# A fixed list of TensorE's products replaced by a choice made step by step, in a fused attention and two-layer kernel

## The chip, the cores and the metric

The kernel runs on one core of a Trainium2 chip. The metric is device microseconds of one execution, the median of several. Matrix products run on TensorE (PE), elementwise work on VectorE (DVE), ScalarE (ACT) and GpSimd (POOL), and transfers are issued by SyncE (SP).

## What is computed

Three stages stand behind one another, with 2304 tokens (4 batches of 576), 8 heads of 64 and a model width of 512:

```python
kv  = einsum('bhsd,bhse->bhde', k, v)          # linear attention
out = einsum('bhsd,bhde->bhse', q, kv)
x   = out / sqrt(mean(out**2) + 1e-6) * g_norm
x   = ((x @ w_a) * (x @ w_b)) @ w_out          # 512 -> 1536 -> 512
h   = x @ w_in                                 # 512 -> 1024
solu = h * softmax(h)
y   = layernorm(solu) * g_ln @ w_out2          # 1024 -> 512
```

The weights arrive as float64 and are turned into pairs of float32r numbers, high and low, on the chip.

## The kernel before: how the work is ordered

The kernel is written in Python that emits instructions engine by engine. Each engine runs its own queue in the order of emission, so the order in which the Python code calls the helpers is the order on the chip. To choose that order the code keeps a small model of time (`Order`, L45 to L92): every operation is given an assumed duration, every engine a time at which it is free, and chains of operations (`od.chain`) are emitted when the model's clock reaches them. The model sets the order alone. On the chip each instruction waits for its real inputs.

**Attention.** For a batch there are four key-value products (`att_kv`, tiles `pkv`, L468) and five token tiles. A token tile is a product with q (`att_1`, tile `o`, L491), a square on ScalarE (`sq`, L516), a copy (`x`, L508), a sum on VectorE (`r`, L518), a power on GpSimd (`r`, L521), a multiplication on VectorE (`x`, L522), and then a transposition on TensorE (`att_2`, tile `t`, L533) that ScalarE and VectorE copy out as `xh` (L546) and `xl` (L547). The tiles `pkv`, `o` and `t` share two PSUM buffers.

**Weights.** A chunk of w_a, w_b or w_out (512 columns; the three of one `f` are `w f,0`, `w f,1`, `w f,2`) is loaded as int64 into one of three buffers, decoded by one step on ScalarE (L286) and five on VectorE (L289, L292, L298, L303, L307), and split by ScalarE (`wh`, L365) and GpSimd (L366, `wl` L367). There are places for six split chunks, so for two values of `f`.

**First layer.** The width of 1536 is cut into 12 parts `f`, the tokens into six blocks `j` of 384. A block of `f` is eight groups of three products for w_a and w_b (`ab_items`, L563 to L565), an elementwise product `a` on ScalarE and VectorE (L612, L613), a split into `gh` (ScalarE, L615) and `gl` (GpSimd, L616), and four groups of three products with w_out (`y_items`, L643), whose sum goes to `ya`: a copy on ScalarE (L654) or an addition on VectorE (L656).

**Order of the first layer.** Before the change it is a list, `main` (L830 to L841): for each block the products of f=0 and f=1 and then the products with w_out of both, summed in one PSUM tile; from f=2 on one f after the other, the products with w_out of a block behind the next block's first products. The loop (L858 to L906) takes the list's next item when the model says that it is ready, and mixes attention in by a credit that `att_cost` (L847) works out from the attention due for the next block. Loads of weights stand between loads of attention by the table `FIRST` (L197): how many weight chunks may be asked for after how many attention loads.

**Second layer.** It runs behind that as a pipeline over 18 token tiles (`run_h`, `run_t`, `run_o`, L726 to L827), which the change leaves as it is.

Of the kernel before, what the change touches and what calls it, by code (L numbers as in the profile page):

```python
# [9 lines left out]
F32 = mybir.dt.float32  # L10
# [7 lines left out]
P = 128  # L18
# [95 lines left out]
def attention_moe_moe_kernel(ctx: ExitStack, tc, kv_in, kv_tail, q_in, g_norm, w1, w_in, w_out2, g_ln, out):  # L114
# [155 lines left out]

    def rank_of(k):

        return {("w", 0, 0): 1.5, ("w", 0, 1): 1.5, ("w", 0, 2): 2.5, ("w", 1, 0): 2.5}.get(k, 5)

    def decode(k):
        nm = f"{k[0]}{k[1]}_{k[2]}"
        slot, raw, when = arrived.pop(k)
        su, sf = R_U.take(), R_F.take()
        w = raw.bitcast(U32).rearrange("p (n two) -> p n two", two=2)
        u = ph1.tile([P, CH], F32, tag="u", name="u_" + nm)  # L280
        f = ph1.tile([P, CH], F32, tag="f", name="f_" + nm)
# [13 lines left out]

        def b3():

            nc.vector.scalar_tensor_tensor(  # L298
                out=fb, in0=w[:, :, 1], scalar=0xC0000000, in1=ub, op0=ALU.bitwise_and, op1=ALU.bitwise_or
            )  # L300

        def b4():
            nc.vector.tensor_scalar(out=ub, in0=fb, scalar1=0xFF800000, scalar2=None, op0=ALU.bitwise_and)  # L303

        def b5():

# [12 lines left out]
        od.chain(  # L319
            [("A", 0.52, a), ("V", 0.34, b1), ("V", 0.34, b2), ("V", 0.6, b3), ("V", 0.34, b4), ("V", 0.6, b5),  # L320
             (None, 0, freed), (None, 0, last)],
            rank=rank_of(k), t=max(od.now, when),
        )

    def store(k, f, u, su, sf, t):

        what, x, y = k
        if what == "o" and x >= 3:
            wf[x] = w2.tile([P, CH], F32, tag=f"wf{x}", name=f"wf{x}", bufs=1)

# [23 lines left out]
        if what == "o":  # L354
            g = gl_sb[:, x:x + 1]
            gwh[x], gwl[x] = hi, lo
            ops = [
                ("G", 1.23, lambda: nc.gpsimd.tensor_tensor(out=f, in0=f, in1=u, op=ALU.add)),
                ("A", 0.6, lambda: nc.scalar.activation(out=hi, in_=f, func=AF.Copy, scale=g)),
                ("V", 0.66, lambda: nc.vector.scalar_tensor_tensor(  # L360
                    out=lo, in0=f, scalar=g, in1=hi.bitcast(F32), op0=ALU.mult, op1=ALU.subtract)),
            ]
        else:
            ops = [
                ("A", 0.52, lambda: nc.scalar.copy(out=hi, in_=f)),  # L365
                ("G", 1.23, lambda: nc.gpsimd.tensor_tensor(out=f, in0=f, in1=hi.bitcast(F32), op=ALU.subtract)),  # L366
                ("G", 1.23, lambda: nc.gpsimd.tensor_tensor(out=lo, in0=f, in1=u, op=ALU.add)),  # L367
            ]

        def done(t):  # L370
# [79 lines left out]

    def run_back():
        _, b, t, x, sx = back.pop(0)
        od.pe(0.44, lambda: att_2(b, t, x, sx))

    def att_kv(b, p):
        (slot, t, _), tl = arrived.pop(("kv", b, p)), arrived["tail", b, 0][1]
# [28 lines left out]
    def att_1(b, t):  # L485
# [25 lines left out]
        def done(when):  # L511
# [9 lines left out]
            ("G", 1.65, lambda: nc.gpsimd.tensor_tensor(out=r[0:n], in0=r[0:n], in1=mhalf[0:n], op=ALU.pow)),  # L521
            ("V", 0.6, lambda: nc.vector.tensor_tensor(  # L522
                out=x[0:n], in0=x[0:n], in1=r[0:n].unsqueeze(2).to_broadcast([n, H, D]), op=ALU.mult)),
            (None, 0, done),
        ], rank=rank, t=od.now + 0.88 + 0.2)
# [46 lines left out]
    def ab_items(f, j):  # L572
# [3 lines left out]
        def ready(m, kt):  # L576
            t = w_ready.get(("w", f, m), INF)
            if m == kt == 0:
                t = max(t, tokens_ready((j + 1) * NB), ps_ready())
                if not (R_A.ok() and R_G.ok()):  # L580
                    return INF
            return t

        def run(m, kt):
            started.add(f)
            if m == kt == 0:
                st["slot"], st["ps"] = ps_tile(f"ab{f}_{j}")
# [12 lines left out]
        def post():  # L600
# [5 lines left out]
            def done(t):  # L606
# [2 lines left out]
                g_ready[f, j] = t  # L609

            od.chain([
                ("A", 0.41, lambda: nc.scalar.copy(out=a, in_=ps[:, 0, 0:NB])),  # L612
                ("V", 0.5, lambda: nc.vector.tensor_tensor(out=a, in0=ps[:, 1, 0:NB], in1=a, op=ALU.mult)),  # L613
                ps_done(st["slot"]),
                ("A", 0.41, lambda: nc.scalar.copy(out=gh, in_=a)),  # L615
                ("G", 0.96, lambda: nc.gpsimd.tensor_tensor(out=gl, in0=a, in1=gh.bitcast(F32), op=ALU.subtract)),  # L616
                (None, 0, done),
            ], t=od.now + G3 + 0.1)
# [4 lines left out]
    def y_items(fs, j):  # L623
# [10 lines left out]
        def run(f, m2, i):  # L634
# [198 lines left out]
    n_two = len(main)  # L833
    prev = None
    for f in range(2, NF1):
        for j in range(NBLK):
            main += ab_items(f, j)
            if prev:
                main += y_items(*prev)
            prev = [f], j  # L840
    main += y_items(*prev)  # L841

    n_block = n_two // NBLK
    AHEAD = 4
    SLACK = 3.0

    def att_cost(n):  # L847

        t = 0.44 * sum(b * S + i * P < n for _, b, i, *_ in back)
        for w, b, i in front:  # L850
            if b * S + (i * P if w == "t" else 0) < n:
                t += 1.32 if w == "t" else 0.75
        return t

    loads()
    decode_more()
    credit, n_main = 0.0, 0
    while main:  # L858
        od.until(od.now)
        loads()  # L860
        decode_more()
        if w2 is None and not att_left[0]:
# [6 lines left out]
        cost, ready, run = main[0]  # L869
        can = ready() <= od.now  # L870
        b_can = back and back[0][0] <= od.now and R_PA.ok()
        f_can = front_ready() <= od.now
        if (b_can or f_can) and (credit > 0 or not can):
            t0 = od.now
            after_back[0] = b_can
            if b_can:
                run_back()
            else:
                run_front()
            if can:  # L880
                credit -= od.now - t0
            continue
        if can:
# [7 lines left out]
            main.pop(0)  # L891
            n_main += 1
            od.pe(cost, run)
            split_more()
            continue
        if f_can or b_can:
            continue

        if todo_h and len(main) <= 8 and h_ready(todo_h[0]) <= od.now and len(held) < 2:
            run_h(todo_h.pop(0))  # L900
            continue
        nxt = [t for t in (ready(), front_ready(), back[0][0] if back and R_PA.ok() else INF) if t < INF]
        if od.events:
            nxt.append(od.events[0][0])
        assert nxt, "stuck"
        od.now = max(od.now, min(nxt))  # L906
    while todo_o:
        od.until(od.now)
        ahead = len(todo_o) - len(todo_h)
# [83 lines left out]
```

## Time and profile before

| what | value |
|---|---|
| median of three executions | 742.25 us (742.07 to 742.89) |
| the profiled execution | 742.4 us |
| its span in the profile | 740.5 us |
| TensorE busy | 719.1 us, 97% of the span |
| VectorE, GpSimd, ScalarE busy | 477.2, 283.1, 247.2 us |
| TensorE's granted clock, mean | 0.993 of full speed |

The span is the time from the first to the last instruction on the core. The profiled execution's own time is 1.9 us longer than its span, and that part lies outside what the trace shows. A matmul's busy time covers its whole pass through the array, and passes overlap, so that TensorE can be counted busy while its rate is below the best. The granted clock is given as a share of 2.4 GHz, where 0.50 is 1.2 GHz.

### The profile page before, as it was taken

What the parts mean: (1) busy time and instruction counts of PE and PEld (TensorE: products, weight loads), DVE (VectorE), ACT (ScalarE), POOL (GpSimd) and SP (SyncE); (2) the same over time, 40 slices, a digit from 0 to 9 for tenths busy, and PEclk for the clock granted to TensorE, in tenths of its full rate; (3) what the DMA queues carried; (4) which work ended last, traced back from release to release, by engine and by line L of the source; (5) the groups of instructions that cost most, each with busy time, mean ns of one, the idle gap of its engine ahead of it and who ended that gap; (6) DMA issues with size and microseconds to landing.
All of it is one profiled execution on the core that took longest, in us unless ns stands there. A gap on an engine that the chain in (4) does not pass through costs nothing.

```text
span 740.5 us, 10433 instructions
## 1 busy us (share of the span) xinstructions
PE 719.1 (97%) x4184; PEld 670.9 (91%) x4184; DVE 477.2 (64%) x662; ACT 247.2 (33%) x458; POOL 283.1 (38%) x271
## 2 busy tenths in 40 slices
PE   5799999899999999999999999999999999999998
PEld 5679999889999999999999999999878888888887
DVE  3992554699959595959594939466695544536350
ACT  4574555433333232323231313224532221212221
POOL 2792424575656464535352525221420111111110
PEclk9799999999999999999999999999999999999999
DMA  8715050023121212121211100000000000000001
GB/s 305 284 66 192 23 212 2 29 89 110 58 86 58 86 58 85 58 86 58 86 58 57 58 29 29 1 1 0 1 1 29 26 19 29 14 30 15 28 26 46
DMA packets 16336, 46.81 MB, mean 63 GB/s; under 512 B 2080, under 2 KB 3360, under 8 KB 16288
## 3 DMA queue, kind: packets, MB, share of 16 engines
q1 hardware_dynamic: 16288, 46.15, 17.2%
q8 instruction: 33, 0.54, 0.3%
q14 instruction: 15, 0.12, 0.0%
HBM read 41.42 MB, written 4.72 MB: 62 GB/s over the span
## 4 chain that ended last, share of the span: by engine, by line
PE 87%; DVE 7%; ACT 2%; POOL 2%; issue 2%; DMA 1%; SPq 0%; ACTq 0%; POOLq 0%
PE y L643 18%; PE ab L563 12%; PE ab L564 12%; PE ab L565 12%; PE h L565 4%; PE out L565 4%; PE h L563 4%; PE out L564 4%; PE out L563 4%; PE h L564 4%; PE t L792 2%; PE o L491 2%; PE pkv L468 2%; DMA kv<-in_kv 1%; DVE f_w L298 1%
## 5 line engine op out<-in xcount | busy, mean ns | idle before, releaser
L563 PE MATMUL ab<-xh,wh_w 128*128 128x384 f32 x576 | 195.3, 339 | 0.0
L564 PE MATMUL ab<-xl,wh_w 128*128 128x384 f32 x576 | 193.0, 335 | 0.4 <-DVE xl L547 0.4
L565 PE MATMUL ab<-xh,wl_w 128*128 128x384 f32 x576 | 193.0, 335 | 0.1
L616 POOL TENSOR_TENSOR gl<-a,gh 128x384 fp32r<-128x384 f32 x72 | 75.6, 1050 | 150.9 <-ACT gh L615 150.9
L656 DVE TENSOR_TENSOR ya<-y,ya 128x768 f32<-128x768 f32 x120 | 111.3, 949 | 6.6 <-PE y L643 5.1
L563 PEld LDWEIGHTS ab<-xh,wh_w 128*128 128x128 f32 x576 | 108.5, 188 | 1.0 <-issue 0.3
L564 PEld LDWEIGHTS ab<-xl,wh_w 128*128 128x128 f32 x576 | 108.5, 188 | 0.8 <-DVE xl L547 0.8
L565 PEld LDWEIGHTS ab<-xh,wl_w 128*128 128x128 f32 x576 | 108.4, 188 | 0.4 <-POOL wl_w L367 0.4
L643 PE MATMUL y<-gh,wh_w 128*128 128x384 f32 x288 | 97.7, 339 | 1.9 <-ACT gh L615 1.9
L643 PE MATMUL y<-gl,wh_w 128*128 128x384 f32 x288 | 96.8, 336 | 2.3 <-POOL gl L616 2.2
L613 DVE TENSOR_TENSOR a<-ab,a 128x384 f32<-128x384 f32 x72 | 39.8, 553 | 88.2 <-ACT a L612 88.2
L643 PE MATMUL y<-gh,wl_w 128*128 128x384 f32 x288 | 96.3, 334 | 0.0
L366 POOL TENSOR_TENSOR f_w<-f_w,wh_w 128x512 f32<-128x512 f32 x36 | 50.3, 1396 | 62.3 <-ACT wh_w L365 62.3
L612 ACT COPY a<-ab 128x384 f32<-128x384 f32 x72 | 34.4, 477 | 102.0 <-PE ab L565 101.9
L770 DVE TENSOR_REDUCE st<-h 128x1 f32<-128x1024 f32 x18 | 22.0, 1220 | 67.1 <-PE h L565 67.0
L643 PEld LDWEIGHTS y<-gl,wh_w 128*128 128x128 f32 x288 | 54.1, 188 | 3.6 <-POOL gl L616 3.6
L563 PE MATMUL h<-winh,yh 128*128 128x512 f32 x144 | 56.2, 390 | 0.8 <-DVE u L772 0.8
L643 PEld LDWEIGHTS y<-gh,wh_w 128*128 128x128 f32 x288 | 54.1, 188 | 2.9 <-ACT gh L615 2.6
L565 PE MATMUL h<-winh,yl 128*128 128x512 f32 x144 | 56.2, 391 | 0.0
L564 PE MATMUL h<-winl,yh 128*128 128x512 f32 x144 | 56.1, 389 | 0.0
L643 PEld LDWEIGHTS y<-gh,wl_w 128*128 128x128 f32 x288 | 54.1, 188 | 0.0
L615 ACT CAST gh<-a 128x384 fp32r<-128x384 f32 x72 | 37.0, 513 | 48.2 <-DVE a L613 47.9
(92 smaller groups left out, 1157.4 us busy)
## 6 DMA issues: line engine op xcount, KB each, us to landing
raw_w<-in_w SPq DMA_DIRECT2D x36, 512.0 KB, 3.2
kv<-in_kv SPq DMA_DIRECT2D x16, 512.0 KB, 4.5
out<-ot SPq DMA_DIRECT2D x17, 256.0 KB, 2.0
raw_i<-in_w_in SPq DMA_DIRECT2D x8, 512.0 KB, 3.2
raw_o<-in_w_out SPq DMA_DIRECT2D x8, 512.0 KB, 3.3
q<-in_q SPq DMA_DIRECT2D x12, 288.0 KB, 4.7
tail<-in_kv_tail SPq DMA_DIRECT2D x4, 256.0 KB, 5.4
q<-in_q SPq DMA_DIRECT2D x4, 192.0 KB, 5.0
```

The lines of the kernel that those rows point to most:

```text
L366: ("G", 1.23, lambda: nc.gpsimd.tensor_tensor(out=f, in0=f, in1=hi.bitcast(F32), op=ALU.subtract)),
L468: nc.tensor.matmul(o, lhsT=k, rhs=v, start=c == 0, stop=c == SC)
L563: nc.tensor.matmul(o, lhsT=ah, rhs=bh, start=first, stop=False)
L564: nc.tensor.matmul(o, lhsT=ah, rhs=bl, start=False, stop=False)
L565: nc.tensor.matmul(o, lhsT=al, rhs=bh, start=False, stop=last)
L612: ("A", 0.41, lambda: nc.scalar.copy(out=a, in_=ps[:, 0, 0:NB])),
L613: ("V", 0.5, lambda: nc.vector.tensor_tensor(out=a, in0=ps[:, 1, 0:NB], in1=a, op=ALU.mult)),
L615: ("A", 0.41, lambda: nc.scalar.copy(out=gh, in_=a)),
L616: ("G", 0.96, lambda: nc.gpsimd.tensor_tensor(out=gl, in0=a, in1=gh.bitcast(F32), op=ALU.subtract)),
L643: nc.tensor.matmul(o, lhsT=x[:, s], rhs=y, start=f == fs[0] and n == 0, stop=f == fs[-1] and n == 2)
L656: op = ("V", 0.87, lambda: nc.vector.tensor_tensor(out=dst, in0=src, in1=dst, op=ALU.add))
L770: ("V", 1.13, lambda: nc.vector.tensor_reduce(out=nmax, in_=ps, axis=AX.XY, op=ALU.max, negate=True)),
```

## The change

The list is gone. The loop now keeps, for each f, the blocks whose products with w_a and w_b are still to do (`ab`), the block begun (`busy`), and a queue `yq` of blocks whose products with w_out are still to do. At each step it takes the next block of the oldest unfinished f, or, where that block is not ready in the model, the next block of the f behind it. The products with w_out come when they are ready and two further blocks are behind them, or when nothing else is ready. Attention gets a credit of twice the time of each other item (`ATT`). The products with w_out of f=0 and f=1 are no longer summed in one PSUM tile: f=0 is copied, f=1 is added on VectorE. The buffers of `a` and `gh`/`gl` are claimed at a block's last group and not at its first. The model's durations are new, so are the ranks of the first chunks, and three entries are added to `FIRST` and two moved.

```diff
-    FIRST = {0: 1, 9: 3, 14: 4, 17: 5, 21: 6}
+    FIRST = {0: 1, 9: 3, 14: 4, 18: 5, 22: 6, 27: 7, 32: 8, 36: 9}
...
-        return {("w", 0, 0): 1.5, ("w", 0, 1): 1.5, ("w", 0, 2): 2.5, ("w", 1, 0): 2.5}.get(k, 5)
+        return {("w", 0, 0): 1.5, ("w", 0, 1): 1.5, ("w", 0, 2): 2.5, ("w", 1, 0): 3.5, ("w", 1, 1): 3.5}.get(k, 5)
...
-            [("A", 0.52, a), ("V", 0.34, b1), ("V", 0.34, b2), ("V", 0.6, b3), ("V", 0.34, b4), ("V", 0.6, b5),
+            [("A", 0.6, a), ("V", 0.5, b1), ("V", 0.5, b2), ("V", 0.95, b3), ("V", 0.5, b4), ("V", 0.85, b5),
...
-    G3 = 0.4885
+    G3 = 0.52
...
-                if not (R_A.ok() and R_G.ok()):
-                    return INF
+            if m == 1 and kt == NP - 1 and not (R_A.ok() and R_G.ok()):
+                return INF
...
-                if f < 2:
+                if f < 1:
...
-    G2 = 0.6515
+    G2 = 0.68
...
-    main = []
-    for j in range(NBLK):
-        main += ab_items(0, j) + ab_items(1, j) + y_items([0, 1], j)
...
+    ab = [[ab_items(f, j) for j in range(NBLK)] for f in range(NF1)]
+    yq, busy = [], []
+    ATT = 2.0
+
+    def next_ab():
+
+        if busy:
+            return busy[0]
+        two = [f for f in range(NF1) if ab[f]][0:2]
+        for n, f in enumerate(two):
+            if (n == 0 or len(ab[f]) > len(ab[two[0]])) and ab[f][0][0][1]() <= od.now:
+                busy.append(ab[f].pop(0))
+                yq.append([f, NBLK - 1 - len(ab[f]), None])
+                return busy[0]
+        return None
...
+        a, y = next_ab(), next_y()
+        if a and a[0][1]() > od.now:
+            a = None
+
+        it = y if y and (len(y) < 4 or not a or len(yq) > 2) else a
...
-        if (b_can or f_can) and (credit > 0 or not can):
+        if (b_can or f_can) and (credit > 0 or not it):
...
+            c, ready, run = it.pop(0)
             if att_left[0]:
-
-                j = n_main // n_block
-                credit += cost * max(
-                    att_cost((j + 2) * NB) / max(G3 * (n_block - n_main % n_block) - SLACK, G3),
-                    att_cost(NT) / max(G3 * (n_two - n_block - n_main), G3),
-                )
...
+                credit += ATT * c
```

What this moves is seen in the engines' queues. **ScalarE, third and fourth token tile of batch 0** (`sq_3`, `x_3`: the fourth tile's square and copy; `xh` out of `t_0`: the first tile's transposition). Before:

```order
L516 ACTIVATE sq_3_267<-o_3_261 128x512
L520 ACTIVATE r_2_251<-r_2_251 128x8
L546 ACTIVATE xh_106<-t_0_274,gn 128x4x128
L365 CAST wh_w_1_286<-f_w_1_163 128x512
L508 COPY x_3_266<-o_3_261 128x512
L520 ACTIVATE r_3_268<-r_3_268 128x8
L546 ACTIVATE xh_106<-t_1_294,gn 128x4x128
```

and now:

```order
L516 ACTIVATE sq_3_266<-o_3_260 128x512
L508 COPY x_3_265<-o_3_260 128x512
L520 ACTIVATE r_2_251<-r_2_251 128x8
L546 ACTIVATE xh_106<-t_0_274,gn 128x4x128
L516 ACTIVATE sq_4_288<-o_4_282 64x512
L508 COPY x_4_287<-o_4_282 64x512
L546 ACTIVATE xh_106<-t_1_297,gn 128x4x128
```

The copy `x_3`, which frees a PSUM buffer, stood behind `xh` and a weight split, and stands directly behind `sq_3` now; the split of chunk `w 0,1` goes behind the second tile's `xh`.

**VectorE, second and third token tile of batch 0** (`xl` out of `t_1` and of `t_2`, or `x_2`, `x_3`: the tiles' products with their factors; `u_w_2`, `f_w_2`: decoding of the chunk `w 0,2`). Before:

```order
L547 SCALAR_TENSOR_TENSOR xl_107<-t_1_294,gn,xh_106 128x4x128
L518 TENSOR_REDUCE r_4_308<-sq_4_307 64x8
L298 SCALAR_TENSOR_TENSOR f_w_2_219<-raw_w_2_151,u_w_2_218 128x512
L522 TENSOR_TENSOR x_3_266<-x_3_266,r_3_268 128x512
L547 SCALAR_TENSOR_TENSOR xl_107<-t_2_317,gn,xh_106 128x4x128
```

and now:

```order
L547 SCALAR_TENSOR_TENSOR xl_107<-t_1_297,gn,xh_106 128x4x128
L518 TENSOR_REDUCE r_3_267<-sq_3_266 128x8
L518 TENSOR_REDUCE r_4_289<-sq_4_288 64x8
L289 TENSOR_SCALAR u_w_2_220<-u_w_2_220 128x512
L547 SCALAR_TENSOR_TENSOR xl_107<-t_2_335,gn,xh_106 128x4x128
L292 TENSOR_SCALAR u_w_2_220<-u_w_2_220 128x512
L522 TENSOR_TENSOR x_3_265<-x_3_265,r_3_267 128x512
L298 SCALAR_TENSOR_TENSOR f_w_2_221<-raw_w_2_151,u_w_2_220 128x512
```

The decoding step at L298 and the product `x_3` stood ahead of the third tile's `xl` and stand behind it now.

**TensorE, the last blocks of f=0 and f=1** (`ab_5_1439` is block 5 of f=1 before; `ab_2_1321` and `ab_3_1386` are blocks 2 and 3 of f=1 in the change; `y_5` and `y_2` are products with w_out of those blocks, or of block 5 of f=0). Before:

```order
L565 MATMUL ab_5_1439<-xh_109,wl_w_1_487 128x384
L643 MATMUL y_5_0_1481<-gh_5_1433,wh_w_2_372 128x384
...
L643 MATMUL y_5_1_1495<-gh_5_1433,wl_w_2_373 128x384
L643 MATMUL y_5_0_1481<-gh_5_1478,wh_w_2_553 128x384
...
L563 MATMUL ab_0_1532<-xh_106,wh_w_0_1416 128x384
```

and now:

```order
L565 MATMUL ab_2_1321<-xh_106,wl_w_1_663 128x384
L644 MATMUL y_5_0_1364<-gh_5_1293,wh_w_2_432 128x384
...
L644 MATMUL y_5_1_1373<-gh_5_1293,wl_w_2_433 128x384
L563 MATMUL ab_3_1386<-xh_109,wh_w_0_521 128x384
...
L644 MATMUL y_2_0_1422<-gh_2_1361,wh_w_2_741 128x384
```

Before, 12 products lay between the end of f=1's last block and the first product that reads its `gh` (`gh_5_1478`). Now 12 products with w_out of another set and the 24 of a further block lie between a block and its own products with w_out.

Two counts hold for the whole queue of TensorE. Its first 588 instructions (as they are issued) are the same set before and after: all attention, f=0 and f=1 whole, and block 0 of f=2. From instruction 589 on, block 1 of f=2, the order is the same to the end.

## Rows read from the trace of the kernel before

**Rows 1.** The page's head and its part 1, TensorE's line.
```profile
span 740.5 us, 10433 instructions
...
PE 719.1 (97%) x4184; PEld 670.9 (91%) x4184; DVE 477.2 (64%) x662; ACT 247.2 (33%) x458; POOL 283.1 (38%) x271
```

**Rows 2.** The chain that ended last, blocks of y: start us, us, what.
```profile
182.65 2.08 PE y L643 x12
...
519.61 2.08 PE y L643 x12
```

**Rows 3.** Busy time by stretch: us, busy (instructions) of each engine, PEclk, DMA share, GB/s.
```profile
20.00:54.00 34.00, 28.88 (x220) 23.84 (x218) 33.18 (x46) 20.50 (x48) 28.59 (x19) 0.85 0.48 175
```

**Rows 4.** TensorE in order of time: start us, us, instruction, [idle before it].
```profile
22.23 0.66 PE L533 MATMUL t<-ident,x 128*128 128x128 f32 x4 [1.77 <-ACT x L508]
...
25.79 1.11 PE L533 MATMUL t<-ident,x 128*128 128x128 f32 x4 [1.75 <-DVE xl L547]
...
29.34 0.69 PE L564 MATMUL ab<-xl,wh_w 128*128 128x384 f32 x1 [0.35 <-DVE xl L547]
...
143.61 0.45 PE L643 MATMUL y<-gh,wh_w 128*128 128x384 f32 x1 [1.54 <-ACT gh L615]
...
150.91 0.33 PE L563 MATMUL ab<-xh,wh_w 128*128 128x384 f32 x1
```

**Rows 5.** ScalarE in order of time, tile 3 of batch 0.
```profile
19.79 0.60 ACT L516 ACTIVATE sq<-o 128x512 f32<-128x512 f32 x1 [0.24 <-PE o L491]
...
21.58 0.59 ACT L508 COPY x<-o 128x512 f32<-128x512 f32 x1
```

**Rows 6.** VectorE in order of time, tiles 1 and 2 of batch 0.
```profile
25.00 0.74 DVE L547 SCALAR_TENSOR_TENSOR xl<-t,gn,xh 128x512 fp32r<-128x512 f32 x1
...
28.55 0.73 DVE L547 SCALAR_TENSOR_TENSOR xl<-t,gn,xh 128x512 fp32r<-128x512 f32 x1
```

**Rows 7.** Busy time by stretch, for PEclk, the column behind POOL.
```profile
23.00:24.00 1.00, 1.00 (x8) 0.66 (x7) 0.92 (x2) 0.61 (x1) 1.00 (x2) 0.81 1.01 401
28.00:33.50 5.50, 5.15 (x34) 3.91 (x34) 5.46 (x8) 2.28 (x5) 4.35 (x3) 0.50 0.80 267
33.50:60.00 26.50, 24.90 (x216) 21.24 (x213) 22.07 (x32) 17.23 (x41) 19.73 (x13) 0.99 0.38 135
```

**Rows 8.** TensorE's waits: total us, times, longest us.
```profile
PE t L533 <- DVE xl L547: 2.4, 3, 1.8
PE t L533 <- ACT x L508: 2.3, 2, 1.8
PE y L643 <- POOL gl L616: 2.2, 4, 0.9
PE y L643 <- ACT gh L615: 1.9, 2, 1.5
```

**Rows 9.** Instruction groups: the five VectorE steps that decode one weight chunk.
```profile
L298 DVE SCALAR_TENSOR_TENSOR f_w<-raw_w,u_w 128x512 uint32<-128x512 uint32 x36 | 36.1, 1003 | 0.7
L307 DVE SCALAR_TENSOR_TENSOR u_w<-raw_w,u_w 128x512 f32<-128x512 uint32 x36 | 29.1, 808 | 0.8
L289 DVE TENSOR_SCALAR u_w<-u_w 128x512 f32<-128x512 f32 x36 | 21.7, 603 | 15.1 <-ACT u_w L286 15.0
L292 DVE TENSOR_SCALAR u_w<-u_w 128x512 uint32<-128x512 uint32 x36 | 18.7, 518 | 0.5
L303 DVE TENSOR_SCALAR u_w<-f_w 128x512 uint32<-128x512 uint32 x36 | 18.0, 501 | 0.7
```

**Rows 10.** VectorE in order of time, two products of x with its factor.
```profile
21.39 0.68 DVE L522 TENSOR_TENSOR x<-x,r 128x512 f32<-128x512 f32 x1
...
23.14 1.59 DVE L522 TENSOR_TENSOR x<-x,r 128x512 f32<-128x512 f32 x1
```

**Rows 11.** GpSimd in order of time beside them: powers, then a weight step.
```profile
19.15 3.96 POOL L521 TENSOR_TENSOR r<-r,mhalf 128x8 f32<-128x8 f32 x2 [0.20 <-ACT r L520]
...
22.76 1.43 POOL L366 TENSOR_TENSOR f_w<-f_w,wh_w 128x512 f32<-128x512 f32 x1
```

More of the change, by code (lines that the diff above doesn't have):

```diff
@@ L339, in kept @@
                 scale_more()
-            od.chain([("G", 1.23, keep), (None, 0, kept)], rank=5, t=t)
+            od.chain([("G", 1.32, keep), (None, 0, kept)], rank=5, t=t)
             return
@@ L357, in store @@
             ops = [
-                ("G", 1.23, lambda: nc.gpsimd.tensor_tensor(out=f, in0=f, in1=u, op=ALU.add)),
+                ("G", 1.32, lambda: nc.gpsimd.tensor_tensor(out=f, in0=f, in1=u, op=ALU.add)),
                 ("A", 0.6, lambda: nc.scalar.activation(out=hi, in_=f, func=AF.Copy, scale=g)),
@@ L364, in store @@
             ops = [
-                ("A", 0.52, lambda: nc.scalar.copy(out=hi, in_=f)),
-                ("G", 1.23, lambda: nc.gpsimd.tensor_tensor(out=f, in0=f, in1=hi.bitcast(F32), op=ALU.subtract)),
-                ("G", 1.23, lambda: nc.gpsimd.tensor_tensor(out=lo, in0=f, in1=u, op=ALU.add)),
+                ("A", 0.58, lambda: nc.scalar.copy(out=hi, in_=f)),
+                ("G", 1.32, lambda: nc.gpsimd.tensor_tensor(out=f, in0=f, in1=hi.bitcast(F32), op=ALU.subtract)),
+                ("G", 1.32, lambda: nc.gpsimd.tensor_tensor(out=lo, in0=f, in1=u, op=ALU.add)),
             ]
@@ L452, in run_back @@
         _, b, t, x, sx = back.pop(0)
-        od.pe(0.44, lambda: att_2(b, t, x, sx))
+        od.pe(0.5, lambda: att_2(b, t, x, sx))
     def att_kv(b, p):
@@ L520, in att_1 @@
             ("A", 0.2, lambda: nc.scalar.activation(out=r[0:n], in_=r[0:n], func=AF.Copy, bias=1e-6)),
-            ("G", 1.65, lambda: nc.gpsimd.tensor_tensor(out=r[0:n], in0=r[0:n], in1=mhalf[0:n], op=ALU.pow)),
-            ("V", 0.6, lambda: nc.vector.tensor_tensor(
+            ("G", 1.75, lambda: nc.gpsimd.tensor_tensor(out=r[0:n], in0=r[0:n], in1=mhalf[0:n], op=ALU.pow)),
+            ("V", 0.8, lambda: nc.vector.tensor_tensor(
                 out=x[0:n], in0=x[0:n], in1=r[0:n].unsqueeze(2).to_broadcast([n, H, D]), op=ALU.mult)),
@@ L587, in run @@
                 st["slot"], st["ps"] = ps_tile(f"ab{f}_{j}")
+            if m == 1 and kt == NP - 1:
                 st["a"], st["g"] = R_A.take(), R_G.take()
@@ L611, in post @@
             od.chain([
-                ("A", 0.41, lambda: nc.scalar.copy(out=a, in_=ps[:, 0, 0:NB])),
+                ("A", 0.45, lambda: nc.scalar.copy(out=a, in_=ps[:, 0, 0:NB])),
                 ("V", 0.5, lambda: nc.vector.tensor_tensor(out=a, in0=ps[:, 1, 0:NB], in1=a, op=ALU.mult)),
                 ps_done(st["slot"]),
-                ("A", 0.41, lambda: nc.scalar.copy(out=gh, in_=a)),
+                ("A", 0.45, lambda: nc.scalar.copy(out=gh, in_=a)),
                 ("G", 0.96, lambda: nc.gpsimd.tensor_tensor(out=gl, in0=a, in1=gh.bitcast(F32), op=ALU.subtract)),
@@ L827, in run_o, with next_y @@
         R_D.give(sd)
-    main = []
-    for j in range(NBLK):
-        main += ab_items(0, j) + ab_items(1, j) + y_items([0, 1], j)
[L833 to L853, printed above, removed]
+    ab = [[ab_items(f, j) for j in range(NBLK)] for f in range(NF1)]
[11 more added lines that the diff above has]
+        return None
+    def next_y():
+        if not yq:
+            return None
+        q = yq[0]
+        if q[2] is None:
+            q[2] = y_items([q[0]], q[1])
+        return q[2] if q[2][0][1]() <= od.now else None
     loads()
     decode_more()
-    credit, n_main = 0.0, 0
-    while main:
+    credit = 0.0
+    while any(ab) or busy or yq:
         od.until(od.now)
@@ L868, in attention_moe_moe_kernel @@
             decode_more()
-        cost, ready, run = main[0]
-        can = ready() <= od.now
+        a, y = next_ab(), next_y()
+        if a and a[0][1]() > od.now:
+            a = None
+        it = y if y and (len(y) < 4 or not a or len(yq) > 2) else a
         b_can = back and back[0][0] <= od.now and R_PA.ok()
         f_can = front_ready() <= od.now
-        if (b_can or f_can) and (credit > 0 or not can):
+        if (b_can or f_can) and (credit > 0 or not it):
             t0 = od.now
@@ L879, in attention_moe_moe_kernel @@
                 run_front()
-            if can:
+            if it:
                 credit -= od.now - t0
             continue
-        if can:
+        if it:
+            c, ready, run = it.pop(0)
             if att_left[0]:
-                j = n_main // n_block
-                credit += cost * max(
-                    att_cost((j + 2) * NB) / max(G3 * (n_block - n_main % n_block) - SLACK, G3),
-                    att_cost(NT) / max(G3 * (n_two - n_block - n_main), G3),
-                )
-            main.pop(0)
-            n_main += 1
-            od.pe(cost, run)
+                credit += ATT * c
+            if it is y and not y:
+                yq.pop(0)
+            if it is a and not a:
+                busy.pop(0)
+            od.pe(c, run)
             split_more()
             continue
-        if f_can or b_can:
-            continue
-        if todo_h and len(main) <= 8 and h_ready(todo_h[0]) <= od.now and len(held) < 2:
+        if todo_h and not busy and not any(ab) and len(yq) <= 2 and h_ready(todo_h[0]) <= od.now and len(held) < 2:
             run_h(todo_h.pop(0))
             continue
-        nxt = [t for t in (ready(), front_ready(), back[0][0] if back and R_PA.ok() else INF) if t < INF]
+        nxt = [t for t in (busy[0][0][1]() if busy else INF, yq[0][2][0][1]() if yq else INF, front_ready(),
+                           back[0][0] if back and R_PA.ok() else INF) if od.now < t < INF]
+        nxt += [ab[f][0][0][1]() for f in range(NF1) if ab[f] and od.now < ab[f][0][0][1]() < INF][0:2]
         if od.events:
@@ L906, in attention_moe_moe_kernel @@
         od.now = max(od.now, min(nxt))
+    AHEAD = 4
     while todo_o:
```

## The prediction, made before the change was run

> **What bounds the kernel now.** I read the page's head first, then busy time by stretch, then TensorE's waits, and last the queues in order of time. TensorE is busy for 719.1 of 740.5 us [rows 1], so only time in which it waits, or runs at the lower clock, can be won; the change removes no product. Where it lies is soon seen. From 182.65 to 519.61 us the products with w_out come in 55 groups of twelve, exactly 6.24 us apart [rows 2]: (519.61 - 182.65) / 54 = 6.24, that is 36 products of 0.173 us, without a gap. The order there is the same afterwards, and so is that of the second layer. So the change has to pay in the first 180 us. There, from 20 to 54 us, TensorE is busy for 28.88 of 34 us at a mean clock of 0.85, and VectorE for 33.18 of 34 [rows 3]: VectorE, which decodes weights and normalizes attention tiles, bounds the start.
>
> TensorE's first 588 instructions are one set in both orders, and from the 589th on the orders agree. Before, the 589th began at 150.91 us [rows 4]. The prediction is therefore two questions: by how much earlier it begins, and which waits behind it go.
>
> **The change, part by part.**
>
> Start. Before, the transposition t_1 stood still for 1.77 us until the copy x_3, and t_2 for 1.75 us until the xl of t_1 [rows 4]. ScalarE's copy x_3 began at 21.58 because xh and a weight split came first, though its square had begun at 19.79 and taken 0.60 [rows 5]; with the copy right behind the square the buffer is free about 21.58 - 20.39 = 1.2 us earlier, and the xl of t_1 (25.00) moves up by nearly that, 1.1. Then 28.55 - 25.00 = 3.55 us lie between that xl and the next [rows 6], filled by a sum, a decoding step and x_3. The last two now go behind; a further sum and a short step come in, which leaves about 2.7, or 0.8 less. So the first block's xl product, at 29.34 before [rows 4], comes about 1.9 us sooner, and one more key-value product is done by then. I take **2.0**; the ends are 0 (another link of the chain ends last) and 3.5 (both waits whole, 1.77 + 1.75).
>
> Clock. From 28.0 to 33.5 us the granted clock is 0.50, the lower level of 1.2 GHz, with TensorE busy for 5.15 of 5.5 us; it is 0.99 afterwards [rows 7]. Half of 5.15, or 2.6 us, is lost. The clock fell in the 24th microsecond (0.81 there), behind the two stops of 1.77 and 1.75 and their neighbours. With shorter stops it may stay up or come back sooner; I take **1.2**, near the middle of 0 and 2.6, since nothing in the trace decides it. "TensorE: Matmul & The Clock Gate" of the Trainium skill, Part 1, says that "the default state is throttled, and activity releases the throttle". By that rule alone the whole 2.6 would come back, as the new order leaves shorter gaps there, and the time would be 1.4 us lower than mine; the trace agrees in that the clock fell after gaps, but shows no gap of the new length.
>
> Batches 0 and 1, 28 to 60 us. TensorE's remaining waits for attention are 2.4 - 1.75 = 0.65 for xl, 2.3 - 1.77 = 0.53 for the copy [rows 8], and 0.35 at the first block [rows 4]: **1.5** in all. I expect them gone, as VectorE has less ahead of these tiles: before the last tile of batch 1 it now runs seven decoding steps fewer, the five of one chunk and two of another, 0.60 + 0.52 + 1.00 + 0.81 + 0.50 + 0.81 + 0.50 = 4.7 us [rows 9]. In place of those chunks TensorE works on later blocks of f=0. Ends 0 and 1.5.
>
> Products with w_out. Waits for gl are 2.2 us in four places and for gh 1.9 us in two [rows 8], **4.1** together, the longest 1.54 at 143.61 [rows 4]. Before, twelve products (2.1 us) lay between f=1's last block and its own products with w_out, while VectorE decoded the chunk of f=2 ahead of that block's a. Now 36 products, 6.24 us [rows 2], lie between, and since f=0 finishes ahead of f=1 the weight places come free in two steps. A third of that distance was short by 1.54, so 6.24 is enough. Ends 0 and 4.1.
>
> What is added. f=1's sums become 12 additions on VectorE instead of part of an accumulation; most stand behind 60 us, and their cover is VectorE's slack there (64% busy over the span [rows 1]; if it were gone, a PSUM buffer would come free late). Powers are bunched ahead of the split of f=1's chunks on GpSimd, so the first block of f=1, and ScalarE's and VectorE's tiles queued behind, can be late. The trace has no such wait; the nearest are the six waits on gl and gh, mean 4.1 / 6 = 0.7 us [rows 8]. I take two of them less rounding, **-1.1**; ends 0 and -8.8, all of the gain. The claims of buffers, moved loads and new durations act through the order alone and get nothing of their own: behind the first products TensorE waits for no load, and their cover is the distance between load and use; without it TensorE would wait for loads as it does in the first microseconds.
>
> Sum: 2.0 + 1.2 + 1.5 + 4.1 - 1.1 = **7.7 us**. The profiled execution took 742.4 us, its span 740.5 and 1.9 outside it; 742.4 - 7.7 = 734.7. It is 0.15 above the median of the runs shown, so I predict **734.6**.
>
> **The rivals.**
>
> *Only the late waits go.* The chain square, sum, power, product, transposition sets the start as before, and the first three terms are nothing: 742.4 - 4.1 + 1.1 = 739.4. For it: VectorE is 98% busy from 20 to 54 us [rows 3], and loses only work that it must do later. Against it: the two longest stops of TensorE come from the order of two instructions on ScalarE and VectorE, and that order changes. 16%.
>
> *The clock stays low through the denser attention* (the other side). If 1.2 GHz lasted from 27 us until batch 1 is through near 51, 24 us at half speed, 12 would be lost, 9.4 more than the 2.6 now, and the clock term goes: 742.4 - 7.7 + 1.2 + 9.4 = 745.3. It turns slower when the low stretch is longer than now by twice 6.5, so past about 46 us. For it: attention's products are short and come with stops. Against it: from 33.5 to 60 us, with about 1.6 us idle (26.5 - 24.9), the clock stayed at 0.99 [rows 7]. 8%.
>
> *GpSimd's powers lock out VectorE* (also slower). Beside GpSimd's weight step at 22.76 the product x took 1.59 us instead of 0.68 [rows 10, 11]. But the product at 21.39 took 0.68 while powers ran from 19.15 to 23.11. Were the powers to block too, each 1.98 long, the five of batch 1, now bunched beside its products, would cost 5 x 1.98 = 9.9: 742.4 - 7.7 + 9.9 = 744.6. "SBUF — State Buffer" of the Trainium skill, in its practical consequences on ports, has a VectorE instruction with two SBUF inputs contend with any GpSimd instruction that reads SBUF; the weight step agrees, the power does not, and the measurement decides. 3%.
>
> *New waits eat the gain.* The last term is near its far end: about 742. 8%.
>
> *The clock also holds.* The whole 2.6, no new wait and 3.5 at the start: 742.4 - 11.7 = 730.7. 5%.
>
> **How the numbers follow.** The forecast has the remaining 60%, from about 732 to 738. Less than 0.2%, about 1.5 us, cannot be told from no change here. Faster by more than that: 60 + 16 + 5 = 81%. Within it: 8%. Slower: 8 + 3 = 11%. The range from 731.0 to 741.0 takes in the forecast and the first rival with their bounds, and leaves out some 20%: the slower cases, most of the case without gain, and the best one's end.
>
> **What would show it.** Right: the 589th TensorE instruction starts near 145 us; no wait for gl or gh above half a microsecond; the groups of y 6.24 us apart as before; the first product with xl near 27.4. Each term can be read alone: the start in the waits of t, the clock in its stretch at 0.50, the late waits in those of y. Wrong: the same 150.91 with shorter waits, which would mean that TensorE's rate and not its waits was lost; a low clock past 40 us; new waits of ab on wl, or of y on ya, between 50 and 110 us.

## The result, and the profile after

The changed kernel took 731.9 us (median of four, 731.34 to 732.54) beside 742.16 for the one before on the same chip: ratio 0.986, 95% interval 0.9843 to 0.9877, or 10.3 us less. Predicted were 734.6, with 731.0 to 741.0 as the range. The profiled execution took 731.34 us.

The page's head and part 1, against [rows 1]: the span is 10.9 us shorter, TensorE's busy time 5.2 of that.

```profile
span 729.6 us, 10425 instructions
PE 713.9 (98%) x4184; PEld 669.5 (92%) x4184; DVE 492.2 (67%) x674; ACT 245.6 (34%) x458; POOL 282.7 (39%) x271
```

Busy time by stretch, against [rows 3, 7] (PEclk stands behind POOL). The clock never falls, and where it was at 0.50 TensorE is now full:

```profile
20.00:54.00 34.00, 29.93 (x293) 25.14 (x291) 32.14 (x48) 23.22 (x56) 26.13 (x18) 1.00 0.75 279
28.00:33.50 5.50, 5.50 (x56) 5.00 (x53) 5.38 (x9) 3.95 (x10) 4.50 (x4) 1.00 0.98 367
33.50:60.00 26.50, 24.31 (x216) 21.69 (x217) 25.81 (x34) 18.38 (x43) 20.80 (x14) 1.00 0.64 234
60.00:130.00 70.00, 69.43 (x489) 66.09 (x488) 46.14 (x69) 36.95 (x79) 34.18 (x25) 1.00 0.19 66
```

TensorE in order of time, against [rows 4]. The first product with xl begins at 26.84 (29.34 before), the 589th instruction at 142.42 (150.91). (The 588 ahead of it are rows of the queue; in either trace they are 1016 single instructions.)

```profile
22.29 0.66 PE L533 MATMUL t<-ident,x 128*128 128x128 f32 x4 [0.39 <-DVE xl L547]
...
26.84 0.44 PE L564 MATMUL ab<-xl,wh_w 128*128 128x384 f32 x1 [0.35 <-DVE xl L547]
...
38.62 0.66 PE L533 MATMUL t<-ident,x 128*128 128x128 f32 x4 [0.76 <-ACT x L508]
39.69 1.09 PE L491 MATMUL o<-bd,q 128*64 128x128 f32 x8 [0.41 <-ACT x L508]
...
50.40 0.46 PE L533 MATMUL t<-ident,x 64*128 64x64 f32 x4 [0.99 <-DVE xl L547]
...
142.42 0.33 PE L563 MATMUL ab<-xh,wh_w 128*128 128x384 f32 x1
```

TensorE's waits, against [rows 8]: no wait of y is left, while t still waits 1.4 us for xl and 1.3 for x.

```profile
...
PE t L533 <- DVE xl L547: 1.4, 2, 1.0
PE t L533 <- ACT x L508: 1.3, 2, 0.8
PE o L491 <- ACT x L508: 0.9, 2, 0.5
...
```

VectorE about tiles 1 and 2, against [rows 6, 10]: xl follows xl after 2.33 us instead of 3.55, and the operation that is stretched beside GpSimd now stands behind both:

```profile
22.75 0.68 DVE L522 TENSOR_TENSOR x<-x,r 128x512 f32<-128x512 f32 x1
23.70 0.75 DVE L547 SCALAR_TENSOR_TENSOR xl<-t,gn,xh 128x512 fp32r<-128x512 f32 x1 [0.27 <-ACT xh L546]
...
26.03 0.75 DVE L547 SCALAR_TENSOR_TENSOR xl<-t,gn,xh 128x512 fp32r<-128x512 f32 x1
...
27.50 1.75 DVE L522 TENSOR_TENSOR x<-x,r 128x512 f32<-128x512 f32 x1 [0.38 <-POOL r L521]
```

The chain that ended last has the groups of y 6.24 us apart as in [rows 2]; the one that stood at 519.61 before begins 10.95 us sooner:

```profile
502.42 2.08 PE y L644 x12
508.66 2.08 PE y L644 x12
```

Behind it the second layer begins, at 521.52 before and at 510.58 now, with its first product:

```profile
521.52 0.39 PE L563 MATMUL h<-winh,yh 128*128 128x512 f32 x1
```
```profile
510.58 0.39 PE L563 MATMUL h<-winh,yh 128*128 128x512 f32 x1
```

From the 589th instruction to there the old kernel takes 521.52 - 150.91 = 370.61 us, the new one 368.16. So 8.5 us of the gain lie ahead of that instruction and 2.45 behind it.

### The profile page after: what moved, and what is told of

Its sections match the earlier page's. It is cut to its first block, busy times and chain, and to the rows that moved or that the text cites. A ratio compares the mean times of both kernels' runs of the same rounds, so it can differ in the third digit from the quotient of the medians.

```text
span 729.6 us, 10425 instructions
## 1 busy us (share of the span) xinstructions
PE 713.9 (98%) x4184; PEld 669.5 (92%) x4184; DVE 492.2 (67%) x674; ACT 245.6 (34%) x458; POOL 282.7 (39%) x271
## 4 chain that ended last, share of the span: by engine, by line
PE 92%; DMA 3%; DVE 2%; ACT 1%; SPq 1%; issue 0%; ACTq 0%
PE y L644 20%; PE ab L563 13%; PE ab L564 13%; PE ab L565 13%; PE h L563 5%; PE h L565 5%; PE out L565 5%; PE out L563 5%; PE out L564 4%; PE h L564 4%; PE t L793 2%; DMA tail<-in_kv_tail 1%; PE o L491 1%; PE pkv L468 1%; DMA raw_w<-in_w 1%; PE t L533 1%
## 5 line engine op out<-in xcount | busy, mean ns | idle before, releaser
L617 POOL TENSOR_TENSOR gl<-a,gh 128x384 fp32r<-128x384 f32 x72 | 77.7, 1079 | 190.4 <-ACT gh L616 190.2
L657 DVE TENSOR_TENSOR ya<-y,ya 128x768 f32<-128x768 f32 x132 | 125.2, 952 | 8.0 <-PE y L644 5.1
L366 POOL TENSOR_TENSOR f_w<-f_w,wh_w 128x512 f32<-128x512 f32 x36 | 48.6, 1349 | 38.1 <-ACT wh_w L365 38.1
L367 POOL TENSOR_TENSOR wl_w<-f_w,u_w 128x512 fp32r<-128x512 f32 x36 | 51.7, 1436 | 1.8
```

What stands on the lines that cost most here:

```text
L366: ("G", 1.32, lambda: nc.gpsimd.tensor_tensor(out=f, in0=f, in1=hi.bitcast(F32), op=ALU.subtract)),
L367: ("G", 1.32, lambda: nc.gpsimd.tensor_tensor(out=lo, in0=f, in1=u, op=ALU.add)),
```

## The experiments

The theory: two separate gains. The new durations bring another order of attention at the start; the new rule takes away the late waits for gl and gh. The rivals: one of the two does all; the clock is a gain of its own; the load table and ranks carry the start; the distance of two sets is what counts.

**First and fifth: the clock alone.** Spare products in the kernel before, 14 and then 20.

```diff
...
+    def fill(n):
+        for _ in range(n):
+            nc.tensor.matmul(spare[:, 0, 0:P], lhsT=ident, rhs=ident, start=True, stop=True)
...
+        if (b, t) == (0, 0):
+            fill(7)
...
```

> The kernel before, with 14 spare products of the identity with itself (128 columns, into a PSUM tile that nothing reads yet) put where TensorE stopped twice in batch 0 of the attention: 7 behind t of tile 0, 7 behind o of tile 4. Nothing else moves. Theory A (the low clock has a price of its own, because TensorE bounds the start): the granted clock of 28 to 33.5 us is 1.00 instead of 0.50, and the 2.6 us come back, 739.6 us (739 to 740.5). Theory B (VectorE's and GpSimd's chain bounds the start, TensorE at half clock only fills its waiting time): the clock is 1.00 and the time stays at 742.2 (741.5 to 743). Theory C (the spare products do not keep the clock): 0.50 again in that stretch, 742 to 743.

> The kernel before with the 14 spare products of the first experiment and 6 more ahead of the first product with xl, where TensorE stood 1.65 us in that experiment and its clock then fell to 0.50 until about 33.3. Theory B, as that run had it (VectorE's chain bounds the start): the clock is 1.00 throughout, the first product with xl begins at 29.3 again, and the time falls by 0.5 us at most, 741.7 to 742.3. Theory A (behind 29.3 TensorE bounds): the 3.9 us that were at half clock come back as 1.9 us, 740.4 (739.8 to 741).

Measured: 742.32 us (ratio 1.0001, 0.9991 to 1.001) and 742.63 (1.0002, 0.9993 to 1.0011). In the first run the clock stayed at 1.00 until TensorE stood 1.65 us, then fell to 0.50:

```profile
29.34 0.44 PE L573 MATMUL ab<-xl,wh_w 128*128 128x384 f32 x1 [1.65 <-DVE xl L556]
```
```profile
28.00:33.50 5.50, 4.16 (x30) 3.44 (x31) 5.46 (x8) 1.84 (x4) 4.71 (x3) 0.69 0.93 319
```

In the fifth it was 1.00 throughout. Its stretches:

```profile
28.00:33.50 5.50, 5.19 (x49) 4.51 (x48) 5.47 (x7) 2.30 (x5) 4.94 (x3) 1.00 0.90 297
33.50:60.00 26.50, 23.18 (x204) 19.24 (x202) 22.05 (x33) 16.42 (x39) 19.14 (x13) 1.00 0.36 129
```

and TensorE there:

```profile
29.54 0.44 PE L577 MATMUL ab<-xl,wh_w 128*128 128x384 f32 x1 [0.31 <-DVE xl L556]
...
34.72 0.46 PE L540 MATMUL t<-ident,x 64*128 64x64 f32 x4 [0.95 <-DVE xl L556]
```

TensorE does the same work faster and then waits: the product with xl does not come sooner (29.54 against 29.34), a wait of 0.95 for xl is new, and from 33.5 to 60 it idles 3.3 us instead of 1.6. Theory B holds: in the old order VectorE's chain bounds the start, and the low clock lay in TensorE's spare time. The interval is 0.7 us to either side, so in the old order the clock is not worth the 1.2 us of the forecast.

**Second and third: durations alone, rule alone.** The second is the kernel before with every duration of the change and nothing else; the third the changed kernel with the old ones.

```diff
-            [("A", 0.52, a), ("V", 0.34, b1), ("V", 0.34, b2), ("V", 0.6, b3), ("V", 0.34, b4), ("V", 0.6, b5),
+            [("A", 0.6, a), ("V", 0.5, b1), ("V", 0.5, b2), ("V", 0.95, b3), ("V", 0.5, b4), ("V", 0.85, b5),
...
-    G3 = 0.4885
+    G3 = 0.52
...
```

> The kernel before with the new durations alone in the planner (no new rule, load table or ranks). Its order on ScalarE in batch 0 is that of the changed kernel, its late order (two chunks mixed, products with w_out behind 12 others at the end of chunk 1) that of before. Theory A (start from the durations, late waits from the rule): the start gains about 5 us (2.5 by the earlier x of tile 3, 2.6 by the clock that does not fall), the waits of 2.2 for gl and 1.9 for gh stay: 737 us (736 to 738.5), clock 1.00 from 28 to 33.5. Rival 1 (the durations do all of it): 732. Rival 2 (the rule does all of it): 742.

> The changed kernel with the old durations put back (new rule, load table and ranks kept). Its order on ScalarE in batch 0 is that of before, its late order that of the changed kernel. Theory A: the clock falls to 0.50 about 28 us again and x of tile 3 comes late, so the start's 5 us are lost; the waits for gl and gh do not come back: 737 us (736 to 738.5). Rival 1 (durations do all): 742. Rival 2 (rule does all): 732.

Measured: durations alone 745.88 (1.0043, 1.0028 to 1.0058), slower, against all three expectations; rule alone 736.76 (0.9918, 0.9903 to 0.9933), as the theory had it. The second's stretch behind the start, and its waits of y:

```profile
33.50:60.00 26.50, 19.87 (x174) 17.30 (x175) 22.48 (x31) 14.56 (x36) 16.85 (x11) 0.87 0.53 189
```
```profile
PE y L643 <- POOL gl L616: 2.4, 5, 0.8
PE y L643 <- ACT gh L615: 1.5, 1, 1.5
```

Its first product with xl came 2.8 us sooner than before; then 6.6 us of 26.5 were idle.

```profile
26.55 0.44 PE L564 MATMUL ab<-xl,wh_w 128*128 128x384 f32 x1 [0.35 <-DVE xl L547]
```

So the start's gain does come from the durations, and under the old list it is lost by 60 us. Which link of the list loses it was not separated. In the third run no wait of y is left, and the start is that of before (1.77 and 1.66 us of stops, first product with xl at 28.99). The second view has that product and the 589th instruction:

```profile
28.00:33.50 5.50, 5.14 (x33) 4.08 (x32) 5.46 (x8) 2.72 (x7) 3.97 (x3) 0.51 0.84 291
```
```profile
28.99 0.69 PE L564 MATMUL ab<-xl,wh_w 128*128 128x384 f32 x1 [0.35 <-DVE xl L547]
...
146.90 0.33 PE L563 MATMUL ab<-xh,wh_w 128*128 128x384 f32 x1
```

So, by the ratios, rule -6.1 us, durations +3.2, both together -10.4: under the new rule the durations are worth 4.3, under the old one they cost 3.2. (The third run has the new load table and ranks, the second the old ones; the seventh shows what these are worth.) The traces say the same by place. In the third run the 589th instruction begins at 146.90 and the second layer 368.16 us later, as in the changed kernel: the rule gives 4.0 us ahead of that instruction and all of the 2.45 behind it. The durations give the other 4.5, from 146.90 to 142.42, all ahead of it.

**Fourth and sixth: one set behind instead of two.**

```diff
-        it = y if y and (len(y) < 4 or not a or len(yq) > 2) else a
+        it = y if y and (len(y) < 4 or not a or len(yq) > 1) else a
```

and for the sixth also

```diff
-                g_ready[f, j] = t
+                g_ready[f, j] = t + 1.0
```

> The changed kernel with products with w_out up to one set behind instead of two (a wait for a set's product then has one set of 24 products, some 4.2 us, to lie under, against about 3.2 us from the last product to gl's end as the trace shows it). Theory A (one set is cover enough): no wait for gl or gh above 0.5 us, 731.9 (731.3 to 732.5). Rival (the second set is what takes the waits away, or the attention uses the room): a wait for gl comes back, 1 to 2 us, 733 to 734.

> The changed kernel with products with w_out up to one set behind, as the fourth experiment (750.5), and the planner told that gl is ready 1.0 us later than it works out. Theory A (one set behind lost because the order placed a set's products where the planner had gl too early, each stop costing its 0.4 us of idle and about 0.3 more): no stop for gl above 0.1 us is left, 732 (731.3 to 733.5). Rival (one set behind loses by something else: PSUM tiles, VectorE's additions, the attention's place): 736 or more, with stops of another kind.

Measured: 750.47 us (1.0103, 1.0088 to 1.0118), 18.6 above the changed kernel, and 731.22 (0.9851, 0.9836 to 0.9866). I had read "one set behind" as a distance of 24 products. It is none: a set counts from its first product on, so its predecessor's y may begin as soon as the model has gl ready, and the model has it too early. The fourth run's waits, and one of its groups:

```profile
PE y L644 <- POOL gl L617: 9.3, 25, 0.9
```
```profile
202.65 0.34 PE L644 MATMUL y<-gh,wh_w 128*128 128x384 f32 x1
203.31 0.45 PE L644 MATMUL y<-gl,wh_w 128*128 128x384 f32 x1 [0.33 <-POOL gl L617]
...
205.36 0.33 PE L563 MATMUL ab<-xh,wh_w 128*128 128x384 f32 x1
```

The group takes 205.36 - 202.65 = 2.71 us instead of 2.08, so a stop that shows 0.33 us of idle costs 0.63: 0.3 are lost beside it. The product ahead of the stop counts as busy for its whole pass of 0.34 us, where the next one otherwise begins after 0.17, and the product behind the stop is followed more slowly. 25 stops give 9.3 + 25 x 0.3 = 16.8 of the 19.4 us by which the span is longer; of the 2.6 that are left, 1.1 is a new stop for a load of q, and the rest was not followed. With gl planned 1.0 us later no such wait is left, and one set behind is as good as two.

**Seventh: load table and ranks of before** (`FIRST` and `rank_of` put back, the rest changed).

> The changed kernel with the load table and the ranks of before (new rule and durations kept). Theory A (rule and durations carry the gain): 732 (731 to 733.5). Rival (the load table and ranks carry the start, some 4.5 us, because weights of chunk 1 come at other times): 736 to 738, with waits of the attention between 33 and 66 us.

Measured: 732.23 us (0.9854, 0.9837 to 0.987). They are worth nothing that can be measured.

**Eighth: keys first.**

```diff
-    FIRST = {0: 1, 9: 3, 14: 4, 18: 5, 22: 6, 27: 7, 32: 8, 36: 9}
+    FIRST = {0: 0, 5: 1, 9: 3, 14: 4, 18: 5, 22: 6, 27: 7, 32: 8, 36: 9}
```

> The changed kernel with one change of its load table: the first weight tile is loaded behind the first five attention loads instead of ahead of all. Theory A (the start hangs on the arrival of the first keys, at 5.4 us): the first products begin about 1.6 us earlier, near 3.9 us, and the end comes 1 to 1.6 us earlier, 730.5 (730 to 731.2). Rival 1 (the first weight tile, now later, holds up the first products with xh): 732 to 734. Rival 2 (the earlier start is swallowed by VectorE's chain around 20 to 27 us): 731.9.

Measured: 737.51 us (0.9932, 0.9917 to 0.9946), a miss by all three. The first key-value product begins 1.1 us sooner, but the next ones wait for their loads, and the fourth is 1.0 us late; in the changed kernel it began at 11.46:

```profile
4.34 1.12 PE L468 MATMUL pkv<-kv 128*64 128x64 f32 x16 [4.34 <-DMA kv<-in_kv]
...
7.96 1.12 PE L468 MATMUL pkv<-kv 128*64 128x64 f32 x16 [2.09 <-DMA kv<-in_kv]
...
12.46 1.12 PE L468 MATMUL pkv<-kv 128*64 128x64 f32 x16 [1.50 <-DMA kv<-in_kv]
```

That is 1.0 of the 5.6 us lost. The first product with xl is already 2.7 us late, at 29.57, and what adds to the delay on the way there was not followed.

**Ninth and tenth: what holds the old start.** The ninth is the third experiment with GpSimd's two steps for the chunk `w 0,1` planned 1.0 us later, which puts its subtraction behind the power of tile 3; the tenth is the third with only the six decoding durations new.

```diff
+        if k == ("w", 0, 1):
+            def rest(t):
+                od.chain(ops[1:] + [(None, 0, done)], rank=rank_of(k) - 0.01, t=t + 1.0)
+
+            od.chain(ops[:1] + [(None, 0, rest)], rank=rank_of(k) - 0.01, t=t)
+            return
```

> The third experiment (new rule, old durations, 736.8) with one step put later: GpSimd's subtraction f_w of the second weight tile comes behind the power of tile 3 instead of ahead of it; TensorE's order is the same row for row, and eight rows in all move on the other engines. Theory A (the start is held by VectorE operations stretched beside GpSimd's 128x512 subtractions): the x product of tile 2, which took 1.60 us beside that subtraction, takes 0.68; the first product with xl begins about 0.9 us earlier than 28.99, and the time is 735.9 (735.2 to 736.3). Rival 1 (the stretch moves on to the next VectorE operation): 28.9 again and 736.8. Rival 2 (the stretch has nothing to do with that subtraction): 1.60 again.

> The third experiment (new rule, old durations, 736.8) with one group of durations new again: those of the six steps that take a weight tile apart (0.52, 0.34, 0.34, 0.60, 0.34, 0.60 to 0.60, 0.50, 0.50, 0.95, 0.50, 0.85). By the order, x of tile 3 then stands right behind its square on ScalarE, as in the changed kernel. Theory A (these six numbers alone put the start right): the first product with xl near 26.5 to 27, the clock at 1.00 from 24 to 33.5, 732 (731 to 733.5). Rival (the other durations are needed too): 735 to 737.

Measured: 736.36 us (0.9917, 0.9902 to 0.9932) and 736.76 (0.9929, 0.9909 to 0.9948). VectorE and GpSimd in the ninth:

```profile
23.06 0.69 DVE L528 TENSOR_TENSOR x<-x,r 128x512 f32<-128x512 f32 x1
...
24.67 1.59 DVE L528 TENSOR_TENSOR x<-x,r 128x512 f32<-128x512 f32 x1
```
```profile
19.09 5.39 POOL L527 TENSOR_TENSOR r<-r,mhalf 128x8 f32<-128x8 f32 x3 [0.21 <-ACT r L526]
24.45 1.26 POOL L366 TENSOR_TENSOR f_w<-f_w,wh_w 128x512 f32<-128x512 f32 x1
```

Moving the subtraction took the stretch from one x product and gave it to the next, as the first rival said; the first product with xl came at 28.65, and the time cannot be told from the third's. Here the stretch belongs to the 128x512 subtraction, not to the powers. The tenth has x of tile 3 right behind its square and a clock of 1.00, yet its first product with xl is at 27.99, and from 33.5 to 60 us TensorE stands idle for 4.4 us:

```profile
33.50:60.00 26.50, 22.13 (x207) 19.01 (x206) 20.02 (x31) 18.08 (x44) 16.09 (x12) 1.00 0.61 230
```

The six numbers alone do not do it; the rest of the durations is needed too. Two of its four executions took 734.94 and 735.49 at a mean clock of 1.0 and 0.999, two 738.02 and 738.18 at 0.995 and 0.993.

**Eleventh: old loads and ranks, gl later.** The edits of the sixth and seventh together, with two sets.

> The changed kernel with the load table and ranks of before (seventh experiment, 732.2) and gl planned 1.0 us later (as in the sixth). Theory A: the one stop for gl left in the seventh experiment (0.8 us at 41 us) goes with its 0.3 behind it, nothing else moves, 731.1 (730.3 to 731.7), a little below the changed kernel. Rival (the order around it changes and the attention's stops of 33 to 66 us come back): 732 to 733.

Measured: 731.13 us (0.9848, 0.9833 to 0.9862). The wait for gl went, and one of 1.6 for x came at 41.57. It is the lowest median of all, but its interval overlaps that of the changed kernel: none of these beats it measurably.

**Twelfth: attention less urgent** (`ATT = 2.0` to `ATT = 0.5`).

> The changed kernel with attention credited at 0.5 of the products' time instead of 2.0, so that it is spread over more products (by the order the last t of the last batch goes from row 282 or so to row 399). Theory A (attention first is worth little: its 2.7 us of stops between 38 and 66 us are chains of one tile behind the other, and spreading them hides them): 730.5 (729.5 to 732). Rival (tokens come late, and products with the first two chunks run out): 733 to 737.

Measured: 735.78 us (0.9909, 0.9895 to 0.9924), slower by 3.9 than the changed kernel, so attention first matters. The loss lies in one stretch, where TensorE does 2.9 us less than after the change:

```profile
33.50:60.00 26.50, 21.39 (x197) 18.25 (x196) 25.05 (x35) 17.64 (x41) 18.99 (x13) 1.00 0.55 211
```

## Why the prediction came out

Direction and range held, and the two questions it was reduced to were the right ones: the 589th instruction began 8.5 us sooner (142.42, for the 145 named), and waits for gl and gh behind it give the other 2.45 of the span's 10.9. The sum of 7.7 was 2.6 short, and its terms were less right than the sum: the batches, which brought nothing, made up for part of what the other four had too low. That it came this near is in part luck.

- **Products with w_out, 4.1: right mechanism, too small.** No y waits any more, and the rule alone, which does this, is worth 6.1 (5.0 to 7.2 by its interval). The term counted idle only. With 0.3 lost beside each of the six stops it is 4.1 + 6 x 0.3 = 5.9; the three of them behind the 589th instruction show 0.39 + 0.92 + 0.30 = 1.6 us of idle and cost 2.45. This is the term that was mis-sized. That the distance of 36 products is the cure was not quite it: the sixth experiment is as fast with y coming whenever gl is ready.
- **Start, 2.0: right, a little small.** The first product with xl came 2.5 us sooner, at 26.84 for the 27.4 named, and for the reason given: the decoding step and x of tile 3 now stand behind the second xl. What it did not name is that some 2 us of this chain were stretch beside GpSimd's weight steps: x of tile 2 ahead of the first of these xl, beside a subtraction (1.59 for 0.68, [rows 10, 11]), and the decoding step between the two, beside an addition, 1.76 in the trace of before where the same step takes 0.68 at 29.18 after. The new order has neither stretch ahead of the second xl. The step and the addition before:

```profile
26.25 1.76 DVE L298 SCALAR_TENSOR_TENSOR f_w<-raw_w,u_w 128x512 uint32<-128x512 uint32 x1
```
```profile
26.20 1.28 POOL L367 TENSOR_TENSOR wl_w<-f_w,u_w 128x512 fp32r<-128x512 f32 x1
```

- **Clock, 1.2: not a term of its own.** It was priced as half of what ran at 0.50 [rows 7]. The clock came back whole, and so far the rule from "TensorE: Matmul & The Clock Gate" of the Trainium skill, Part 1, was nearer than the forecast. But the fifth experiment has the same clock without any gain: in the old order TensorE was not what others waited for. In the new order TensorE is full from 28.0 to 33.5, and there the clock seems to be worth more than 1.2. Of the 4.5 us between the third run and the change at the 589th instruction, 28.99 - 26.84 = 2.15 are there at the first product with xl; from 33.5 to 60 the two idle alike (2.4 and 2.2 us); so most of the other 2.3 must come between, where the clock is 0.51 in the one and 1.00 in the other. Executions point the same way: the seventh kernel took 730.35 us at a mean clock of 1.000 and 732.18 to 732.57 at 0.998, the sixth 730.71 to 731.53 at 1.000 and 732.99 at 0.998. No edit tested it. The prediction also had the clock fall behind both long stops; at 0.81 from 23 to 24 us [rows 7] it was falling before the second began, at 25.79 - 1.75 = 24.04.
- **Batches 0 and 1, 1.5: wrong.** The waits did not go. Idle from 33.5 to 60 is 2.2 us, before 1.6 [rows 7], with stops of 0.76, 0.41 and 0.99. The premise held: ahead of the x of batch 1's last tile VectorE was busy for 42.7 us before and for 35.0 now. But that x comes 8.6 us sooner, at 49.01, and batch 1's products now fall beside GpSimd's work. Three of the five are stretched, to 1.48, 1.52 and 1.80 us, where before all five took 0.67 to 0.92. From 45.59 VectorE runs without a break to the xl that the stop of 0.99 waited for, and 1.80 + 1.77 - 2 x 0.68 = 2.2 us of that are stretch; the other two stops wait for ScalarE's copies.

```profile
45.59 1.80 DVE L522 TENSOR_TENSOR x<-x,r 128x512 f32<-128x512 f32 x1 [0.20 <-POOL r L521]
47.32 1.77 DVE L298 SCALAR_TENSOR_TENSOR f_w<-raw_w,u_w 128x512 uint32<-128x512 uint32 x1
...
49.61 0.73 DVE L547 SCALAR_TENSOR_TENSOR xl<-t,gn,xh 128x512 fp32r<-128x512 f32 x1
```
```profile
45.52 1.63 POOL L521 TENSOR_TENSOR r<-r,mhalf 64x8 f32<-64x8 f32 x1
47.12 1.41 POOL L367 TENSOR_TENSOR wl_w<-f_w,u_w 128x512 fp32r<-128x512 f32 x1
```

The twelfth shows that this stretch, not the first 30 us, is where a less lucky order loses some 3 us; in the tenth 2.2 of its 3.6 us lie there and 1.2 ahead of the first product with xl.

- **Added waits, -1.1: did not come.** There is no stop for gl, and the twelve further additions lie where VectorE is busy for 46.14 of 70 us, which was the cover named.

Start, clock, batches and added waits together were forecast at 3.6; the durations under the new rule are worth 4.3. Of the rivals, late waits alone (739.4) is what the third experiment built; it took 736.8, because the late waits cost more than they show and the added ones did not come. The rival that the clock also holds (730.7, given 5%) is nearer to 731.9 than the forecast: the clock was full and no new wait for gl came, but the start gave 2.5 of its 3.5 and the batches nothing. The slow clock did not occur. Powers that lock out VectorE did not occur as priced: x took 0.69 beside the powers and 1.59 beside the subtraction in the ninth. Yet the x at 45.59 in the changed kernel took 1.80, though by the profile a power alone stood beside it until 47.12; why is open. The rule of "SBUF — State Buffer" of the Trainium skill, in its practical consequences on two SBUF inputs, agrees with the subtraction; it does not agree with most of the powers.

## What to carry to other kernels

Where a planner emits the order, its durations and its rule are one change: here the better durations alone made the kernel slower, and with a rule that may take other ready work they were worth 4.3 us. Count a stop of TensorE between products as its idle plus some 0.3 us beside it, and before pricing a low clock fill the gaps with spare products to see whether TensorE is what bounds; the answer holds for that order alone. Where a consumer is placed by a modelled ready time, a model that is early by less than 1 us costs stops (25 in the fourth run); adding 1 us to the model did as well as more distance.

## What the runs showed of the hardware that was not expected

- A stop of 0.33 us ahead of a 128x384 product cost 0.63 us in all. Beside each of the fourth run's stops, of 0.14 to 0.92 us, the loss was 0.27 to 0.41 us more than the idle.
- The length of the last stop did not decide whether the granted clock fell. It fell to 0.50 behind one stop of 1.65 us in the first experiment (1.00 from 24 to 29, 0.50 from 30 to 33), and behind one of 0.96 in the sixth. It stayed at 1.00 through a stop of 1.87 in the tenth and one of 2.01 in the twelfth. With stops of at most 0.53 us from 20 to 28 it stayed at 1.00 in the changed kernel. The sixth and the twelfth:

```profile
28.89 1.12 PE L468 MATMUL pkv<-kv 128*64 128x64 f32 x16 [0.96 <-DMA kv<-in_kv]
```
```profile
28.00:33.50 5.50, 4.61 (x36) 4.31 (x37) 3.65 (x7) 2.45 (x7) 2.35 (x2) 0.69 0.99 385
```
```profile
53.35 0.46 PE L533 MATMUL t<-ident,x 64*128 64x64 f32 x4 [2.01 <-DVE xl L547]
```
```profile
50.00:54.00 4.00, 1.47 (x13) 1.03 (x12) 3.97 (x5) 1.26 (x5) 2.01 (x2) 1.00 0.95 338
```

- A 128x512 subtraction on GpSimd stretched a VectorE product of two SBUF tiles from 0.69 to 1.59 us, wherever it was moved; three 128x8 powers in a row did not. One product that began 0.07 us behind a power did take 1.80 us (at 45.59 in the changed kernel; 1.78 to 1.80 in the second, fourth and sixth run).
